# Decode block with adaptive norm: the last weights cut into five transfers, and the first norm worked in columns

## The chip, the cores and the metric

The kernel runs on one core of one Trainium2 chip. The metric is the device time of one execution in microseconds (us): 699.27 us before the change, the median of three runs (698.72 to 700.05). All data is float32. The four compute engines are called PE (TensorE, matrix products), DVE (VectorE), ACT (ScalarE) and POOL (GpSimd); SP (SyncE) issues the transfers.

## The reference

One decode step (one new token) for a batch of two: attention over a cache of 4096 positions with 32 heads of width 128, then a two-layer network with the Mish activation. Each half stands behind a layer norm whose shift, scale and output gate come from a condition `c`.

```python
mod = (_silu(c) @ w_mod).reshape(c.shape[0], 6, 1, -1)
sa, ca, ga, sb, cb, gb = (mod[:, i] for i in range(6))
h = _layernorm(x) * (1 + ca) + sa
x = x + ga * _A_ref(h, k_cache, v_cache, wq, wo)   # softmax(q k / sqrt(128)) v, then wo
h = _layernorm(x) * (1 + cb) + sb
x = x + gb * _B_ref(h, w1, b1, w2)                 # mish(h w1 + b1) w2
```

The caches are 2 x 32 x 4096 x 128 numbers each, 268 of the 297 MB that the kernel reads. `w_mod` is 512 x 3072, `wq` 512 x 4096, `wo` 4096 x 512, `w1` 512 x 1376 and `w2` 1376 x 512.

## The kernel before

**Transfers.** All large loads are issued by SP into three rooms of 64 KB per partition (tag `room0` to `room2`), which take turns. The first is `first` (L83): the modulation's weights for five of the six vectors and the bias `b1`. Then come `wq` (L86), the keys of head 0 (L87), 31 transfers for the heads (L89 to L95; most hold the keys of one head and the values of an earlier one), `wo` (L97), the values of heads 29 and 30 in the room named `two` (L102), then `last` (L107: the values of head 31 in two parts, the rest of `wo`, and `w1` in two halves), and at the end `tail` (L123). `tail` holds the weights of the output gate's modulation `gb` and those of the second layer, `w2`, in 11 chunks of 128 rows; it comes in four transfers, in the order of `src["w2"]`: the gate's modulation with chunks 0 to 4, chunks 5 to 7, chunks 8 and 9, and chunk 10 (`_lay_out`, L635 to L639). A room is loaded again as soon as its last reader is through: `used` (L152) issues the next entry of `plan` when what it holds has been read. The room of `tail` is that of `two`, so its issue waits for the value product of head 30 (`values(H - 2)`, L486). A small transfer `cx` (L73) brings condition and input as 16 rows of 128 numbers on ACT's queue, beside `first`.

**Start.** Two products with an identity (L264, L267) turn `cx` into columns (feature on the partition, `cps`) and into rows at a spacing of 32 partitions (`xq`). The condition goes through silu into `ct` (L269 to L273). The first norm works on rows, with its mean and variance summed over partitions by two products with `mean_w` (`centred`, `rstd`, L204 to L229). `modulation` (L236) multiplies `ct` with the weights in `first`: three vectors (L284), then two (L291). Scale and shift are applied on rows (L286, L287), and `columns` turns the result into `ht` (L288). The queries follow when `wq` is there (L308).

**Heads.** For each head DVE multiplies keys by the query (L336) and sums (L340), PE and ACT do the softmax over partitions, and PE multiplies the weights with the values (L382) in the accumulators `ov`.

**End.** After the last head's values, `wo` is applied (L491), the second norm and the first layer run (L502 to L546), and the hidden layer collects in `fps` (L559). Then PE's order is: the gate's modulation (L568), four products that keep PE busy and whose result nobody reads (`idle(4)`, L569), and 44 products of the second layer in the order of the chunks (L585). DVE and ACT make the activation `actt` from `fps` meanwhile (L572 to L580), multiply the result `yps` by the gate (L593) and add the residual (L594), and SP stores it.

```python
    x2_rows = keep("x2", x2ps)
    gps = modulation("5", 0, 1, w_t["mod5"])
    idle(4)
```

Of the kernel before, what the change touches and what calls it, by code (L numbers as in the profile page):

```python
# [8 lines left out]
F32 = mybir.dt.float32  # L9
BF16 = mybir.dt.bfloat16  # L10
# [4 lines left out]
P = 128  # L15
B = 2
# [14 lines left out]
WO_FIRST = H - 2  # L31

# [12 lines left out]
def kernel(ctx: ExitStack, tc: tile.TileContext, src: dict, out: bass.AP):  # L45
# [26 lines left out]
    cx = const.tile([16, P], F32, name="cx")  # L72
    nc.scalar.dma_start(out=cx, in_=src["cx"])  # L73

# [10 lines left out]
    b1_early = first[:, G * 5 * D :]  # L85
# [66 lines left out]
    def used(*items):  # L152
# [37 lines left out]
    busy = const.tile([P, 512], BF16, name="busy")  # L190
    for t in (ct, ht, h2t, x2t, *(t for pair in e_t for t in pair), busy):
        nc.gpsimd.memset(t, 0.0)
# [11 lines left out]
    def centred(s):  # L204
        rs = const.tile([P, 8], F32, name="rs")
        xc = const.tile([P, P], F32, name="xc")
        sq = const.tile([P, P], F32, name="sq")
        nc.vector.tensor_reduce(out=rs[:, 0:1], in_=s, axis=AX.X, op=ALU.add)
        mps = small_ps("mean_a")
        nc.tensor.matmul(mps[:, 0:1], lhsT=mean_w, rhs=rs[:, 0:1], start=True, stop=True)  # L210
        nc.vector.tensor_scalar(out=xc, in0=s, scalar1=mps[:, 0:1], scalar2=None, op0=ALU.subtract)
        nc.vector.scalar_tensor_tensor(
            sq, xc, 1.0, xc, op0=ALU.mult, op1=ALU.mult, accum_out=rs[:, 1:2]
        )
        vps = small_ps("var_a")
        nc.tensor.matmul(vps[:, 0:1], lhsT=mean_w, rhs=rs[:, 1:2], start=True, stop=True)
        return xc, vps[:, 0:1], rs

    def rstd(var, rs):
        nc.scalar.activation(rs[:, 2:3], var, AF.Ln, bias=eps_t[:, 0:1])  # L220
        nc.vector.tensor_scalar(out=rs[:, 4:5], in0=var, scalar1=EPS, scalar2=None, op0=ALU.add)
        nc.scalar.activation(rs[:, 3:4], rs[:, 2:3], AF.Exp, scale=-0.5)
        nc.vector.scalar_tensor_tensor(
            rs[:, 5:6], rs[:, 3:4], rs[:, 4:5], rs[:, 3:4], op0=ALU.mult, op1=ALU.mult
        )
        nc.vector.tensor_scalar(
            out=rs[:, 5:6], in0=rs[:, 5:6], scalar1=-0.5, scalar2=1.5, op0=ALU.mult, op1=ALU.add
        )
        return rs[:, 3:4], rs[:, 5:6]  # L229
# [28 lines left out]
    def idle(n):  # L258
        for _ in range(n):
            nc.tensor.matmul(ov[1], lhsT=busy[:, 0:P], rhs=busy, start=True, stop=True)  # L260


    cps = small_ps("cps")[:, : 2 * G * B]
    nc.tensor.matmul(cps, lhsT=cx, rhs=ident[0:16, 0 : 2 * G * B], start=True, stop=True)  # L264
    cps, xtps = (cps[:, G * B * i : G * B * (i + 1)].rearrange("p (g b) -> p g b", b=B) for i in range(2))
    xps0 = small_ps("xps0")[:, :P]
    nc.tensor.matmul(xps0, lhsT=place.rearrange("p g r -> p (g r)"), rhs=cx, start=True, stop=True)  # L267
    sg = const.tile([P, G, B], F32, name="sg")
    nc.scalar.activation(sg, cps, AF.Exp, scale=-1.0)  # L269
    nc.vector.tensor_scalar(out=sg, in0=sg, scalar1=1.0, scalar2=None, op0=ALU.add)  # L270
    nc.vector.reciprocal(sg, sg)
    nc.vector.tensor_tensor(out=ct[:, :, 0:B], in0=cps, in1=sg, op=ALU.mult)
    nc.vector.tensor_copy(two(ct)[:, :, B - 1], ct[:, :, B - 1])  # L273
    xt = small("xt")
    nc.vector.tensor_copy(xt, xtps)
    xq = const.tile([P, P], F32, name="xq")
    nc.vector.tensor_copy(xq, xps0)

    xn = const.tile([P, P], F32, name="xn")
    xc, var, rs = centred(xq)  # L280
    y0, y1 = rstd(var, rs)
    nc.vector.tensor_scalar(out=xn, in0=xc, scalar1=y0, scalar2=y1, op0=ALU.mult, op1=ALU.mult)

    ps = modulation("0", 0, 3, w_t["mod"])  # L284
    hq = const.tile([P, P], F32, name="hq")
    nc.vector.scalar_tensor_tensor(hq, ps[:, 1, :], 1.0, xn, op0=ALU.add, op1=ALU.mult)  # L286
    nc.vector.tensor_tensor(out=hq, in0=ps[:, 0, :], in1=hq, op=ALU.add)  # L287
    hps = columns(hq, "hps")  # L288
    nc.vector.tensor_copy(ht[:, :, 0:B], hps)
    ga = keep(2, ps[:, 2, :])  # L290
    ps = modulation("3", 3, 2, w_t["mod"])  # L291
    sb, cb = keep(3, ps[:, 0, :]), keep(4, ps[:, 1, :])
    gat, cbt, scale_t = small("gat"), small("cbt"), small("scale_t")
# [174 lines left out]
    def whole(t, name):  # L468
        ps = small_ps(name)[:, : G * B]
        nc.tensor.matmul(ps, lhsT=ones, rhs=t, start=True, stop=True)  # L470
        s = const.tile([P, B], F32, name=name)
        nc.vector.tensor_reduce(
            out=s, in_=over_g(ps.rearrange("p (g b) -> p g b", b=B)), axis=AX.X, op=ALU.add
        )
        return s

# [12 lines left out]
    for i in range(2):  # L489
# [11 lines left out]
    u, x2, xm, sq2 = small("u"), two(x2t), small("xm"), small("sq2")  # L501
    nc.vector.tensor_tensor(out=u, in0=xps, in1=scale_t, op=ALU.mult)  # L502
    nc.vector.tensor_tensor(out=h2t[:, :, 0:B], in0=u, in1=offset, op=ALU.add)
    nc.vector.tensor_tensor(out=xm, in0=xps, in1=gat, op=ALU.mult)
    nc.vector.tensor_tensor(out=x2, in0=xm, in1=xt, op=ALU.add)
    x_sum = whole(x2, "x_sum")
    nc.vector.scalar_tensor_tensor(
        xm, each_g(x_sum), -1.0 / D, x2, op0=ALU.mult, op1=ALU.add
    )
    nc.vector.tensor_tensor(out=sq2, in0=xm, in1=xm, op=ALU.mult)  # L510
# [16 lines left out]
    v_sum = whole(sq2, "v_sum")  # L527
    for k in range(1, G):
        first_layer(k)
    st = const.tile([P, 6, B], F32, name="st")  # L530
    nc.scalar.activation(st[:, 0], v_sum, AF.Ln, bias=eps_t[:, 0:1], scale=1.0 / D)
    nc.scalar.activation(st[:, 1], st[:, 0], AF.Exp, scale=-0.5)
    nc.vector.tensor_scalar(
        out=st[:, 2], in0=v_sum, scalar1=-0.5 / D, scalar2=-0.5 * EPS, op0=ALU.mult, op1=ALU.add
    )
    nc.vector.scalar_tensor_tensor(st[:, 3], x_sum, 1.0 / D, near, op0=ALU.mult, op1=ALU.subtract)
    coef = small("coef")
# [123 lines left out]
```

## Time and profile before

| | before |
|---|---|
| median of three runs | 699.27 us (698.72 to 700.05) |
| the profiled execution, its own time | 698.93 us |
| its span, first to last instruction | 697.2 us |
| read from memory | 297.23 MB, 426 GB/s over the span |
| DVE busy | 587.6 us (84%) |
| PE busy | 292.9 us (42%) |
| ACT, POOL busy | 39.5 us (6%), 4.7 us (1%) |

The span is the time between the first and the last instruction of the profiled execution. The run's own time has 1.7 us more, which lie around the span. A busy share is a mean over the whole span; where the end of the kernel is set by one chain of work, the chain and the stretch around it say more than the share. Bytes in transit are shown as the mean busy share of the core's 16 DMA engines.

### The profile page before, as it was taken

What the parts mean: (1) busy time and instruction counts of PE and PEld (TensorE: products, weight loads), DVE (VectorE), ACT (ScalarE), POOL (GpSimd) and SP (SyncE); (2) the same over time, 40 slices, a digit from 0 to 9 for tenths busy, and PEclk for the clock granted to TensorE, in tenths of its full rate; (3) what the DMA queues carried; (4) which work ended last, traced back from release to release, by engine and by line L of the source; (5) the groups of instructions that cost most, each with busy time, mean ns of one, the idle gap of its engine ahead of it and who ended that gap; (6) DMA issues with size and microseconds to landing.
All of it is one profiled execution on the core that took longest, in us unless ns stands there. A gap on an engine that the chain in (4) does not pass through costs nothing.

```text
span 697.2 us, 4054 instructions
## 1 busy us (share of the span) xinstructions
PE 292.9 (42%) x1679; PEld 100.6 (14%) x1680; DVE 587.6 (84%) x240; ACT 39.5 (6%) x187; POOL 4.7 (1%) x22
## 2 busy tenths in 40 slices
PE   2360435432350435443504453444322453443886
PEld 1110101110110101111101111111100111110244
DVE  3039999999899999999999999999999899999102
ACT  1000000000000000000000000000000000000000
POOL 2000000000000000000000000000000000000000
PEclk9775565666655666566655558665765566556879
DMA  9999999999999999999999999999999999999996
GB/s 407 406 448 425 432 456 429 422 429 440 445 429 425 426 440 440 432 430 416 446 440 430 432 432 437 432 429 440 429 433 432 426 440 432 433 432 413 434 418 252
DMA packets 6686, 297.49 MB, mean 427 GB/s; under 512 B 756, under 2 KB 780, under 8 KB 1292
## 3 DMA queue, kind: packets, MB, share of 16 engines
q1 hardware_dynamic: 6636, 297.23, 98.8%
q8 instruction: 13, 0.21, 0.1%
q14 instruction: 5, 0.04, 0.0%
q10 hardware_dynamic: 32, 0.01, 0.0%
HBM read 297.23 MB, written 0.00 MB: 426 GB/s over the span
## 4 chain that ended last, share of the span: by engine, by line
DMA 49%; DVE 45%; PE 5%; issue 0%; ACT 0%; SPq 0%; DVEq 0%
DMA kv<-in_pair 40%; DVE kv L336 22%; DVE s L340 21%; DMA two<-in_single 4%; PE ov L382 2%; DMA tail<-in_w 2%; DMA first<-in_mod 2%; PE modps L241 1%; DVE n L358 1%; DVE n L357 1%; PE yps L585 0%; PE otp L398 0%; PE att L422 0%; PE last_ps L463 0%; DVE m L350 0%
## 5 line engine op out<-in xcount | busy, mean ns | idle before, releaser
L336 DVE TENSOR_TENSOR kv<-kv,qb 128x8192 f32<-128x8192 f32 x32 | 277.9, 8684 | 44.2 <-DMA kv<-in_pair 22.5
L340 DVE TENSOR_REDUCE s<-kv 128x64 f32<-128x8192 f32 x32 | 277.4, 8667 | 0.0
L382 PE MATMUL ov<-kv,e 128*32 128x512 f32 x928 | 168.6, 893 | 5.2 <-ACT e L366 5.2
L362 PE MATMUL mb<-n,ones 2*128 2x2 f32 x64 | 17.7, 344 | 221.4 <-DVE n L358 221.4
L321 PE MATMUL qb<-q_sb,row_of 32*128 32x512 f32 x32 | 28.4, 1035 | 65.4 <-DVE kv L336 65.4
L382 PEld LDWEIGHTS ov<-kv,e 128*32 128x32 f32 x928 | 36.9, 156 | 118.7 <-issue 109.6
L362 PEld LDWEIGHTS mb<-n,ones 2*128 2x128 f32 x64 | 15.8, 303 | 230.3 <-issue 155.5
L352 PE MATMUL mt<-ident,m 128*2 128x128 f32 x64 | 13.7, 300 | 75.8 <-DVE m L350 75.8
L363 ACT COPY m<-mb 128x2 f32<-128x2 f32 x32 | 5.1, 160 | 532.2 <-PE mb L362 423.7
L366 ACT ACTIVATE e<-s,m 128x32 f32<-128x32 f32 x64 | 20.0, 314 | 1.2
L321 PEld LDWEIGHTS qb<-q_sb,row_of 32*128 32x128 f32 x32 | 8.8, 302 | 73.7 <-DVE kv L336 67.8
L352 PEld LDWEIGHTS mt<-ident,m 128*2 128x2 f32 x64 | 3.1, 82 | 97.4 <-DVE m L350 76.7
L410 DVE RECIPROCAL total<-l 128x8 f32<-128x8 f32 (+1 forms) x9 | 1.7, 184 | 14.7 <-PE l L408 14.7
L308 PE MATMUL qps<-wq,ht 128*32 128x512 f32 x64 | 9.5, 761 | 10.5 <-DMA wq<-in_wq 10.5
L366 ACT ACTIVATION_READ_ACCUMULATOR e<-s,m 128x1 f32 x64 | 11.9, 186 | 0.0
L398 PE MATMUL otp<-pick,o 128*128 128x8 f32 (+1 forms) x72 | 9.5, 258 | 3.9 <-ACT o L394 3.9
L382 PE MATMUL ov<-two,e 128*32 128x512 f32 x64 | 9.7, 763 | 0.3 <-DMA two<-in_single 0.3
L422 PE MATMUL att<-wo,ot 128*2 128x512 f32 x60 | 9.6, 742 | 0.4 <-DVE ot L401 0.3
L398 PEld LDWEIGHTS otp<-pick,o 128*128 128x128 f32 x72 | 8.7, 191 | 5.5 <-ACT o L394 5.5
L401 DVE TENSOR_TENSOR ot_last<-otp,total 128x4 f32<-128x4 f32 x1 | 0.2, 163 | 11.0 <-PE otp L398 11.0
L357 DVE TENSOR_REDUCE n<-mt 2x1 f32<-2x128 f32 x32 | 8.7, 272 | 0.5 <-PE mt L352 0.5
L394 ACT COPY o<-ov 128x512 f32<-128x512 f32 x9 | 5.3, 586 | 61.4 <-PE ov L382 61.4
(140 smaller groups left out, 107.2 us busy)
## 6 DMA issues: line engine op xcount, KB each, us to landing
kv<-in_single SPq DMA_DIRECT2D x3, 4096.0 KB, 31.1
two<-in_single SPq DMA_DIRECT2D x2, 4096.0 KB, 34.3
wo<-in_wo SPq DMA_DIRECT2D x1, 7680.0 KB, 39.1
first<-in_mod SPq DMA_DIRECT2D x1, 5132.0 KB, 15.1
last<-in_single SPq DMA_DIRECT2D x1, 3072.0 KB, 27.6
last<-in_w SPq DMA_DIRECT2D x2, 1376.0 KB, 34.7
tail<-in_w SPq DMA_DIRECT2D x1, 2304.0 KB, 16.2
last<-in_single SPq DMA_DIRECT2D x1, 1024.0 KB
```

Of the source, the lines that this page charges most:

```text
L241: nc.tensor.matmul(ps[R * g : R * (g + 1)], lhsT=ct[:, k, :], rhs=t[:, k, :].rearrange("p (m n) -> p m n", m=n)[:, :, P * g : P * (g + 1)] ...
L308: nc.tensor.matmul(ps[R * g : R * (g + 1)], lhsT=ht[:, k, :], rhs=w_t["wq"][:, k, 512 * c : 512 * (c + 1)], start=(k == 0), stop=(k == G - 1),
L321: nc.tensor.matmul(qb[:, b], lhsT=row_of[R * g : R * (g + 1), b], rhs=q_sb[R * g : R * (g + 1), half], start=True, stop=True,)
L336: nc.vector.tensor_tensor(out=k_t[h], in0=k_t[h], in1=qv, op=ALU.mult)
L340: nc.vector.tensor_reduce(out=s_t[h].rearrange("p b j -> p (b j)"), in_=k_t[h].rearrange("p b j d -> p (b j) d"), axis=AX.X, op=ALU.add,)
L352: nc.tensor.matmul(mps[h], lhsT=m_t[h][:, 0:2], rhs=ident, start=True, stop=True)
L357: nc.vector.tensor_reduce(out=n[:, 0:1], in_=mps[h], axis=AX.X, op=ALU.max, negate=True)
L362: nc.tensor.matmul(bps[:, 0:2], lhsT=ones[0:B, :], rhs=n[:, 1:3], start=True, stop=True)
L366: nc.scalar.activation(e_t[h % 4][b][:, :, lo : lo + 4], s_t[h][:, b].rearrange("p (c m) -> p c m", m=4), AF.Exp, bias=m[:, 2 + b : 3 + b] ...
L382: nc.tensor.matmul(ov[i % 2][R * g : R * (g + 1), :], lhsT=e_t[h % 4][b][:, c, :], rhs=v_t[h][:, b, 4 * c : 4 * c + 4, :].rearrange("p m d ...
L398: nc.tensor.matmul(tps[:, :n], lhsT=o[:, m, :], rhs=pick[:, m, at : at + n], start=(m == 0), stop=(m == 3))
L422: nc.tensor.matmul(att[R * g : R * g + B, :], lhsT=ot[:, B * h : B * (h + 1)], rhs=w_t["wo"][:, h, :], start=(h < G), stop=(h >= H - 2 - G),)
```

## The change

Three things are changed. (1) Condition and input are laid out as 16 columns of `first`; `cx`, its two products and the row tiles go, and POOL copies those columns and `b1` out of the room into `early`. The first norm is done on columns with the helpers that the second norm now shares, and both modulations run before it. (2) `tail` comes in five transfers instead of four: the gate's modulation alone, chunks 0 to 5, chunks 6 to 8, chunk 9 and chunk 10. Chunk 9 is stored in memory as 8 blocks of 17 rows, of which 16 are read, so that its slowest dimension is 8. (3) The four products of `idle(4)` go.

```diff
-    cx = const.tile([16, P], F32, name="cx")
-    nc.scalar.dma_start(out=cx, in_=src["cx"])
...
-    b1_early = first[:, G * 5 * D :]
+    early_in = first[:, G * 5 * D :]
...
         for part in src["w2"]:
+            if len(part.shape) == 3:
+                nc.sync.dma_start(out=t[:, lo : lo + D], in_=part)
+                lo += D
+                continue
             load(t, lo, part)
...
+    def centred(x, x_sum, name):
+        xm, sq = small(f"xm_{name}"), small(f"sq_{name}")
+        nc.vector.scalar_tensor_tensor(xm, each_g(x_sum), -1.0 / D, x, op0=ALU.mult, op1=ALU.add)
+        nc.vector.tensor_tensor(out=sq, in0=xm, in1=xm, op=ALU.mult)
+        return xm, sq
...
+    early = const.tile([P, (NJ + 2) * G * B], F32, name="early")
+    nc.gpsimd.tensor_copy(early, early_in)
+    c_in, xt = (early[:, G * B * i : G * B * (i + 1)].rearrange("p (g b) -> p g b", b=B) for i in range(2))
+    b1 = early[:, 2 * G * B :]
+    sg = small("sg")
+    nc.scalar.activation(sg, c_in, AF.Exp, scale=-1.0)
...
     ps = modulation("0", 0, 3, w_t["mod"])
+    mod = [keep("012", ps)]
     ps = modulation("3", 3, 2, w_t["mod"])
+    mod.append(keep("34", ps))
+
+    h, sq = centred(xt, whole(xt, "x_sum_a"), "a")
+    times_root(root(whole(sq, "v_sum_a"), "a"), h)
+    nc.vector.scalar_tensor_tensor(h, columns(mod[0][:, 1], "caps"), 1.0, h, op0=ALU.add, op1=ALU.mult)
+    nc.vector.tensor_tensor(out=ht[:, :, 0:B], in0=columns(mod[0][:, 0], "saps"), in1=h, op=ALU.add)
...
     gps = modulation("5", 0, 1, w_t["mod5"])
-    idle(4)
...
+    def on_low_engines(w):
+        t = np.zeros((LOW, P // LOW + 1, w.shape[-1]), w.dtype)
+        t[:, : P // LOW] = w.reshape(LOW, P // LOW, -1)
+        return t
...
-        "cx": np.ascontiguousarray(np.concatenate([eight(a["c"]), eight(a["A_x"])])),
-        "mod01234": join(wm[:, :, : 5 * D], b1c),
+        "mod01234": join(wm[:, :, : 5 * D], eight(a["c"]), eight(a["A_x"]), b1c),
...
-        "w2_0": join(wm[:, :, 5 * D :], w2[:, :5]),
-        "w2_1": join(w2[:, 5:8]),
-        "w2_2": join(w2[:, 8:10]),
-        "w2_3": join(w2[:, 10:]),
+        "w2_0": join(wm[:, :, 5 * D :]),
+        "w2_1": join(w2[:, :6]),
+        "w2_2": join(w2[:, 6:9]),
+        "w2_3": on_low_engines(w2[:, 9]),
+        "w2_4": join(w2[:, 10:]),
...
+    src["w2"][3] = src["w2"][3][:, : P // LOW]
```

At the start, PE before the change stands as follows, from the first product to the last one ahead of the queries (`modps` are the two modulations, `hps` the normed input as columns, `gaps`, `cbps`, `sbps` three modulation vectors as columns).

```order
L264 MATMUL cps<-ident,cx 128x16
L267 MATMUL xps_129<-cx,place 128x128
L210 MATMUL mean_a<-rs,mean_w 128x1
L216 MATMUL var_a<-rs,mean_w 128x1
L241 MATMUL modps_158<-first,ct 32x384 x16
L233 MATMUL hps<-ident,hq 128x8
L241 MATMUL modps_183<-first,ct 32x256 x16
L233 MATMUL gaps<-ident,mod_181 128x8
L233 MATMUL cbps<-ident,mod_202 128x8
L233 MATMUL sbps<-ident,mod_200 128x8
```

After the change the same place has nine groups.

```order
L235 MATMUL modps_126<-first,ct 32x384 x16
L235 MATMUL modps_145<-first,ct 32x256 x16
L197 MATMUL x_sum_a<-early,ones 128x8
L197 MATMUL v_sum_a<-sq_a,ones 128x8
L227 MATMUL caps<-ident,mod_143 128x8
L227 MATMUL saps<-ident,mod_143 128x8
L227 MATMUL gaps<-ident,mod_143 128x8
L227 MATMUL cbps<-ident,mod_162 128x8
L227 MATMUL sbps<-ident,mod_162 128x8
```

The four products ahead of the modulation are gone, and the two sums of the first norm and its two vectors as columns (`caps`, `saps`) now follow both modulations.

At the end, PE before the change stands as follows from the last product of the first layer (`busy` stands four times in a row, and three are left out).

```order
L517 MATMUL w1ps<-last,h2t 32x256
L550 MATMUL x2ps<-ident,x2t 32x128 x4
L559 MATMUL last_ps<-coef,last 128x8 x3
L241 MATMUL modps_1575<-tail,ct 32x128 x16
L260 LDWEIGHTS busy
L260 MATMUL ov_126<-busy 128x512
...
L585 MATMUL yps<-tail,last 32x128 x44
```

After the change:

```order
L485 MATMUL w1ps<-last,h2t 32x352
L485 MATMUL w1ps<-last,h2t 32x256
L508 MATMUL x2ps<-ident,x2t 32x128 x4
L517 MATMUL last_ps<-coef,last 128x8 x3
L235 MATMUL modps_1561<-tail,ct 32x128 x16
L542 MATMUL yps<-tail,last 32x128 x44
```

The gate's modulation (`modps`) stays behind the hidden layer's products (`last_ps`), and the second layer (`yps`) follows it at once.

On SP, the last loads stood so before; a name in brackets that begins with DMAHW is one of eight completion semaphores that the loads use in turn, so a wait on it is a wait for the load eight places earlier (and, on `tail_0`, for the room).

```order
L69 DMA last<-in_w 128x2752 x2
L69 DMA tail<-in_w_0 128x4608 [waits DMAHW4_49,DMAHW5_49,DMAHW3_49,PE_49]
L69 DMA tail<-in_w_1 128x1536
L69 DMA tail<-in_w_2 128x1024
L69 DMA tail<-in_w_3 128x512 [waits DMAHW6_49]
L595 DMA out<-y 4x2x128 [waits DMAHW7_49,DVE_49]
```

After the change:

```order
L69 DMA last<-in_w 128x2752 x2
L69 DMA tail<-in_w_0 128x2048 [waits DMAHW3_49,DMAHW4_49,DMAHW2_49,PE_49]
L69 DMA tail<-in_w_1 128x3072
L69 DMA tail<-in_w_2 128x1536
L127 DMA tail<-in_w_3 128x1x512 [waits DMAHW5_49]
L69 DMA tail<-in_w_4 128x512 [waits DMAHW6_49]
L552 DMA out<-y 4x2x128 [waits DMAHW7_49,DVE_49]
```

There is one issue more. The fourth load of `tail` (chunk 9) waits for the first part of `last`, as the fourth did before; the fifth waits for the second part of `last`, which the store `out` waited for before.

## Rows read from the trace of the kernel before

**Rows 1.** Page, slices of the span and the chain that ended last

```profile
DMA  9999999999999999999999999999999999999996
...
DMA 49%; DVE 45%; PE 5%; issue 0%; ACT 0%; SPq 0%; DVEq 0%
```

**Rows 2.** Page, costliest groups: line, busy and mean, idle before and releaser

```profile
L336 DVE TENSOR_TENSOR kv<-kv,qb 128x8192 f32<-128x8192 f32 x32 | 277.9, 8684 | 44.2 <-DMA kv<-in_pair 22.5
```

**Rows 3.** Timeline, start: start us, us, instruction, [idle before <-releaser]

```profile
7.49 0.18 ACT L269 ACTIVATE sg<-cps 128x8 f32<-128x8 f32 x1 [5.04 <-PE cps L264]
...
8.44 0.17 DVE L273 COPY ct<-ct 128x4 f32<-128x4 f32 x1
...
15.85 0.20 POOL L300 COPY b<-first 128x24 f32<-128x24 f32 x1 [11.46 <-DMA first<-in_mod]
...
15.93 4.68 PE L241 MATMUL modps<-first,ct 128*32 128x384 f32 x32 [4.72 <-DMA first<-in_mod]
```

**Rows 4.** Timeline, SP's first issue for a pair, and the query product

```profile
23.72 0.33 SPq L69 DMA_DIRECT2D kv<-in_pair  x1
...
35.30 9.53 PE L308 MATMUL qps<-wq,ht 128*32 128x512 f32 x64 [10.53 <-DMA wq<-in_wq]
```

**Rows 5.** Timeline, second norm: a sum over partitions and its reduction

```profile
683.37 0.60 PE L470 MATMUL v_sum<-sq,ones 128*128 128x8 f32 x2
...
684.00 0.17 DVE L472 TENSOR_REDUCE v_sum<-v_sum 128x2 f32<-128x8 f32 x1 [1.37 <-PE v_sum L470]
```

**Rows 6.** Chain of waits from 660 us on: start us, us, what

```profile
672.92 16.16 DMA tail<-in_w
...
689.22 1.08 PE modps L241 x32
...
690.46 0.81 PE ov L260 x3
691.27 2.58 PE yps L585 x88
...
693.95 0.30 DVE y L593
```

**Rows 7.** Tile tail, its four issues: ns min/median/max, first and last start

```profile
L69 SPq DMA_DIRECT2D tail<-in_w x4: 327/422/430, 672.9 to 674.2; - x4
```

**Rows 8.** DMA issues of the tail: KB each, us from issue to landing

```profile
tail<-in_w SPq DMA_DIRECT2D x1, 2304.0 KB, 16.2
...
tail<-in_w SPq DMA_DIRECT2D x1, 768.0 KB, 17.6
...
tail<-in_w SPq DMA_DIRECT2D x1, 512.0 KB, 18.4
...
tail<-in_w SPq DMA_DIRECT2D x1, 256.0 KB, 18.6
```

**Rows 9.** Waits of SP's queue from 660 us on: us in total, times, longest

```profile
SPq L595 <- DMA last<-in_single: 1.0, 1, 1.0
```

**Rows 10.** Timeline, hidden layer: last product and last activation step

```profile
687.32 0.83 PE L559 MATMUL last_ps<-coef,last 128*128 128x8 f32 x6 [0.34 <-ACT last L556]
...
689.58 0.20 DVE L580 TENSOR_TENSOR last<-f 128x22 f32<-128x22 f32 x1
```

**Rows 11.** Windows: PE, PEld, DVE, ACT, POOL busy (x), PEclk, DMA share, GB/s

```profile
690.60:691.00 0.40, 0.40 (x3) 0.10 (x1) 0.00 (x0) 0.03 (x1) 0.00 (x0) 1.00 0.25 102
...
692.20:692.60 0.40, 0.40 (x24) 0.40 (x20) 0.00 (x0) 0.00 (x0) 0.00 (x0) 1.00 0.03 10
```

**Rows 12.** Page, instruction queue: packets, MB, share of 16 engines

```profile
q8 instruction: 13, 0.21, 0.1%
```

**Rows 13.** DMA queues from 681 to 683.5 us, the same columns

```profile
q8 instruction: 1, 0.02, 2.7%
```

**Rows 14.** Windows as in rows 11, two stretches by granted clock

```profile
681.99:685.40 3.41, 3.41 (x24) 1.71 (x27) 1.74 (x12) 0.50 (x2) 0.00 (x0) 0.50 1.00 424
685.40:697.20 11.80, 6.84 (x153) 5.15 (x145) 1.88 (x9) 1.24 (x6) 0.00 (x0) 1.00 0.41 165
```

More of the change, by code (lines that the diff above doesn't have):

```diff
@@ L189 @@
     ot_last = const.tile([P, 2 * B], F32, name="ot_last")
-    busy = const.tile([P, 512], BF16, name="busy")
-    for t in (ct, ht, h2t, x2t, *(t for pair in e_t for t in pair), busy):
+    for t in (ct, ht, h2t, x2t, *(t for pair in e_t for t in pair)):
         nc.gpsimd.memset(t, 0.0)
@@ L219, in rstd, with whole @@
[L219 to L224, printed above, removed]
-        )
[L226 to L229, printed above, removed]
+    def whole(t, name):
+        ps = small_ps(name)[:, : G * B]
+        nc.tensor.matmul(ps, lhsT=ones, rhs=t, start=True, stop=True)
+        s = const.tile([P, B], F32, name=name)
+        nc.vector.tensor_reduce(
+            out=s, in_=over_g(ps.rearrange("p (g b) -> p g b", b=B)), axis=AX.X, op=ALU.add
+        )
+        return s
@@ L231, in columns, with times_root @@
+    def times_root(st, t):
+        for _ in range(2):
+            nc.vector.tensor_tensor(out=st[:, 2], in0=st[:, 2], in1=st[:, 1], op=ALU.mult)
+        nc.vector.tensor_tensor(out=t, in0=t, in1=each_g(st[:, 1]), op=ALU.mult)
+        nc.vector.scalar_tensor_tensor(t, each_g(st[:, 2]), 1.5, t, op0=ALU.add, op1=ALU.mult)
     def columns(s, name):
@@ L256, in small @@
         return const.tile([P, G, B], F32, name=name)
[L258 to L267, printed above, removed]
@@ L271 @@
     nc.vector.reciprocal(sg, sg)
-    nc.vector.tensor_tensor(out=ct[:, :, 0:B], in0=cps, in1=sg, op=ALU.mult)
+    nc.vector.tensor_tensor(out=ct[:, :, 0:B], in0=c_in, in1=sg, op=ALU.mult)
     nc.vector.tensor_copy(two(ct)[:, :, B - 1], ct[:, :, B - 1])
[L274 to L281, printed above, removed]
@@ new lines @@
+    h, sq = centred(xt, whole(xt, "x_sum_a"), "a")
+    times_root(root(whole(sq, "v_sum_a"), "a"), h)
+    nc.vector.scalar_tensor_tensor(h, columns(mod[0][:, 1], "caps"), 1.0, h, op0=ALU.add, op1=ALU.mult)
+    nc.vector.tensor_tensor(out=ht[:, :, 0:B], in0=columns(mod[0][:, 0], "saps"), in1=h, op=ALU.add)
+    gat, cbt, scale_t = small("gat"), small("cbt"), small("scale_t")
+    nc.vector.tensor_copy(gat, columns(mod[0][:, 2], "gaps"))
+    nc.vector.tensor_scalar(
+        out=cbt, in0=columns(mod[1][:, 1], "cbps"), scalar1=1.0, scalar2=None, op0=ALU.add
+    )
@@ L466 @@
         )
[L468 to L475, printed above, removed]
     xa, offset = small("xa"), small("offset")
@@ L498 @@
             )
-    u, x2, xm, sq2 = small("u"), two(x2t), small("xm"), small("sq2")
+    u, x2, xg = small("u"), two(x2t), small("xg")
     nc.vector.tensor_tensor(out=u, in0=xps, in1=scale_t, op=ALU.mult)
     nc.vector.tensor_tensor(out=h2t[:, :, 0:B], in0=u, in1=offset, op=ALU.add)
[L504 to L510, printed above, removed]
+    nc.vector.tensor_tensor(out=xg, in0=xps, in1=gat, op=ALU.mult)
+    nc.vector.tensor_tensor(out=x2, in0=xg, in1=xt, op=ALU.add)
+    x_sum = whole(x2, "x_sum_b")
+    _, sq = centred(x2, x_sum, "b")
     w1ps = wide_ps("w1ps")
@@ L526 @@
     first_layer(0)
-    v_sum = whole(sq2, "v_sum")
+    v_sum = whole(sq, "v_sum_b")
     for k in range(1, G):
         first_layer(k)
[L530 to L535, printed above, removed]
+    st = root(v_sum, "b")
     nc.vector.scalar_tensor_tensor(st[:, 3], x_sum, 1.0 / D, near, op0=ALU.mult, op1=ALU.subtract)
@@ L654 @@
         ).ap()
-    src["w2"] = [src.pop(f"w2_{i}") for i in range(4)]
+    src["w2"] = [src.pop(f"w2_{i}") for i in range(5)]
+    src["w2"][3] = src["w2"][3][:, : P // LOW]
     out = nc.dram_tensor("out", inputs["A_x"].shape, F32, kind="ExternalOutput").ap()
```

57 lines of the change are left out of this document (12 added, 45 removed).

## The prediction

> **What bounds the kernel now.** I read the page first: the DMA engines are busy in every slice of the span but the last, and the chain that ended last alternates between transfers (49%) and DVE (45%) [rows 1]. Of the two the transfers set the pace: DVE's product over the keys stood idle 44.2 us in all, most of it until a pair had landed [rows 2]. So what leaves the number of bytes alone can only gain or lose at the two ends: before the queue is full, and after it begins to run dry. The next view is the timeline of the start. The modulation begins at 15.93, as soon as `first` has landed, and the queries only at 35.30, when `wq` has landed; PE is idle for 10.53 us before that [rows 3, 4]. The start therefore has room. The last view is the chain at the end: `tail` is issued at 672.92, its first transfer lands 16.16 us later at 689.08, the gate's modulation starts at 689.22 (0.14 us from landing to product), the four unread products hold PE until 691.27, the second layer takes 2.58 us and the multiplication by the gate starts at 693.95, 0.10 us behind the last product [rows 6]. Everything after that is the same in both kernels.
>
> **The start, part by part.** Removed are `cx`, its two products and the row tiles, all before `first` lands: nothing. The condition now arrives with `first`. POOL copies it at 15.85 in 0.20 us (40 columns for 24, taken at the same price). From the start of the exponential to the end of the copy into `ct` it took 7.49 to 8.61, 1.12 us [rows 3]. So the modulation starts at about 17.3 in place of 15.93, 1.4 us late. Both modulations and the release of the room took from 15.93 to 23.72 [rows 3, 4]; the next pair is thus issued at 25.1 instead of 23.72. The queue then still holds the rest of `wq`, which lands only at about 35.2, and the keys of head 0 behind it, so DMA does not notice. The norm on columns follows: two sums over partitions at 0.80 us each (683.37 to 684.17 [rows 5]), and some 12 small steps of DVE and ACT, 0.3 us each with their gaps at the most, 3.6 us. `ht` is ready near 25.1 + 1.6 + 3.6 = 30.3, 5 us ahead of `wq`. Were PE at half its clock all the way, 3 to 4 us more would still fit. I cost the start at 0.0; its cover is the wait for `wq`, and behind that DVE's waits for pairs [rows 2]. The bytes of `cx` move into `first` and are 8 KB either way: 0.0.
>
> **The end, part by part.** First the price of bytes there. The four issues stand 0.43 us apart (672.9 to 674.2 [rows 7]). With the times to landing [rows 8] the four land at 689.1, 673.35 + 17.6 = 690.95, 673.8 + 18.4 = 692.2 and 674.2 + 18.6 = 692.8. 768 KB thus take 1.85 us, or **0.62 us for 256 KB** on 16 engines.
>
> - The gate's weights alone are 1280 KB less than the first transfer before: they land at 689.1 - 5 x 0.62 = 686.0. The hidden layer's products end at 688.15 (687.32 + 0.83 [rows 10]), so the gate's modulation no longer waits and runs from 688.2 to 689.3, in the shade of the activation on DVE, which ends at 689.78 [rows 10].
> - `idle(4)` goes: with its gap before it 0.97 us of PE's time ahead of the second layer (690.30 to 691.27 [rows 6]).
> - Chunks 0 to 5 end 256 KB later than the first transfer did: 689.1 + 0.62 = 689.7. The second layer starts at about 689.85, both operands being there within 0.1 us of one another. A chunk takes 2.58 / 11 = 0.235 us.
> - Chunks 6 to 8 end 768 KB further: 691.6. PE is through with chunk 5 at 691.26, so here is the **new wait**: chunk 6 starts at 691.6 + 0.14 = 691.74, and everything behind it moves with it.
> - Chunk 9, on eight engines, costs these 16 rows in place of 8, 1.24 us, and the other eight nothing. Chunk 10 costs all 0.62 us.
>
> What chunk 9 does depends on which engines are last. Their ends are apart: from 690.6 to 691.0 the mean share is 0.25, work for four of 16, and from 692.2 on it is 0.03 [rows 11]. So a few engines end up to 1.5 us after the rest. One reason shows: 13 blocks of instructions of 16 KB each came through the same engines [rows 12], and one of them held its engine for 2.7% of 16 x 2.5 us, 1.08 us [rows 13]; 13 delays can't be even on 16 engines. No row names the engines. If the late ones are among the eight without chunk 9, chunk 10 lands there at 691.6 + 0.62 = 692.2, and chunk 9 on the others at 691.6 - 1.4 + 1.24 = 691.4; neither is waited for (they are due at 692.45 and 692.68). If the late ones have chunk 9, it lands at 692.8 and chunk 10 at 693.5. These are the two ends of the cost: no wait, or 0.9 us. The rows say this much: on one engine 13 blocks would make 14 us, so they rotate; in a rotation over all 16 none would get more than one, and a lag of 1.5 us is more than one block of 1.08 us. So the rotation seems to pass over fewer engines, perhaps one half of them, some of which got two blocks and the other half none. Which half that is, no row says. I take the one without chunk 9; that is a choice, and its odds are set below.
>
> - Sum: 691.74 + 5 x 0.235 = 692.92, + 0.10 = 693.02 for the gate's product, against 693.95: **0.93 us less**.
>
> The profiled execution (698.93 us) would so take 698.0. The median of the runs shown, 699.27, lies 0.34 us above it; I set the forecast against the median: 698.3.
>
> Two waits are added on SP. The fourth issue waits for the first part of `last`, as before. The fifth waits for its second part, which ended the 1.0 us wait of `out` behind the fourth issue before [rows 9], at about 675.7. Only `out` is queued behind it, and the queue has work until 691: 0.0; it would cost only if that part landed after 691.
>
> [...] No row before shows a transfer on fewer than 16.
>
> **Rivals.**
>
> 1. *The doubled engines are the late ones.* Chunk 10 lands at 693.5, starts at 693.6, and the gate's product at 693.6 + 0.235 + 0.10 = 693.95: nothing gained, **699.3**. For it: every one of the late engines must lie in the half without chunk 9, or its lag counts, and four drawn at random would seldom do so. Against it: a lag of more than one block speaks for a rotation over a part of the engines [rows 11, 13]. [...] Chance 0.28.
> 2. *Slower: the clock falls without the four products.* They were wide and stood right ahead of the second layer. [...] If it falls again before 689.85, the second layer takes 2 x 2.58 = 5.16 us, ends at 695.0, and the gate's product is at 695.1: 1.2 us more, **700.4**. It decides if the clock is 0.5 for over half of the second layer; from 691.74 on it would cost 1.2 us for five chunks and eat up the gain. Against it: PE had nothing to do from 688.15 to 689.22 before, and the clock held; that gap is now filled, and the new ones are 0.5 us. Chance 0.08.
> 3. *Chunk 9 is spread over all 16 after all.* All lands at 692.8 as before, chunk 10 starts at 692.94, the product is at 693.27: 0.68 us less, **698.6**. Chance 0.08.
>
> **How the numbers follow.** A measurement of this kernel can tell about 0.2%, 1.4 us, from no change. The forecast, 698.3, has 0.49; its own range is 697.8 to 698.8, from chunks 6 to 8 landing 0.4 us earlier or later and the scatter of the medians. Another 0.07 is for what I don't see. The second layer can't start before the activation at 689.78, so the most to be had is 693.95 - (689.85 + 2.58 + 0.10) = 1.4 us; that is why faster by over 0.2% has only 0.13. Slower by over 0.2% needs rival 2 with an unlucky scatter: 0.07. The rest, 0.80, is within 0.2%. For 8 in 10 the range takes in rivals 1 and 3 with their scatter and leaves out rival 2: 697.6 to 699.9.
>
> **What would show it.** In the changed kernel's profile: the modulation near 17.3, `ht` before 31, the query product still at 35.3; the gate's modulation at 688.2 without a wait for DMA; the second layer from 689.85 with a wait for `tail` in its middle and none at its end; the gate's product near 693.0, with the clock at 1.0 in the 3 us before it; fewer engines idle before 691. A wait at the second layer's end is rival 1, a layer of 5 us rival 2. The forecast is wrong if the transfers themselves end at another time, if the queries move, or if the second layer starts after 690.5.

## The result, and the profile after

The change makes the kernel slower by an amount that only many runs can tell: 700.47 us (699.49 to 702.14, 20 runs) against 698.87 us for the kernel before on the same chip (698.61 to 700.50, 20 runs), a ratio of 1.0019 with an interval of 1.0012 to 1.0026. The forecast was 698.3 with a range up to 699.9. The profiled execution took 700.56 us and its span 698.8 us; before it was 698.93 and 697.2, so the profile carries the same 1.6 us as the medians. The times of both kernels fall into two groups, before at 698.4 to 699.3 us (93 of 126 executions in all) and 700.0 to 700.6, after at 699.5 to 699.7 (6 of 20) and 700.2 to 702.1, and the two profiles are of unlike groups: between like ones the loss is 0.4 to 0.7 us, and the rest is that more executions fall into the upper group.

The page's lines on engines, instruction queue, bytes and the chain that ended last:

```profile
PE 290.4 (42%) x1674; PEld 100.1 (14%) x1674; DVE 585.3 (84%) x235; ACT 39.7 (6%) x186; POOL 4.3 (1%) x21
...
q8 instruction: 13, 0.21, 0.1%
...
HBM read 297.23 MB, written 0.00 MB: 425 GB/s over the span
...
DMA 55%; DVE 42%; PE 2%; issue 0%; ACT 0%; SPq 0%; POOL 0%; DVEq 0%
```

The bytes and the 13 blocks of instructions are the same as before [rows 12]. The chain is now 55% transfers, where it was 49% [rows 1]: it ends in a transfer, where the old one ended in PE's work. The timeline, first at the start, then from the issue of `tail` on (start us, us, instruction, idle before and its releaser):

```profile
16.11 0.22 POOL L254 COPY early<-first 128x40 f32<-128x40 f32 x1 [12.21 <-DMA first<-in_mod]
...
17.60 6.37 PE L235 MATMUL modps<-first,ct 128*32 128x384 f32 x64 [17.60 <-DVE ct L262]
...
24.07 20.32 SPq L69 DMA_DIRECT2D kv<-in_pair  x2
...
27.14 0.17 DVE L272 TENSOR_TENSOR ht<-saps,xm_a 128x8 f32<-128x8 f32 x1
...
35.46 8.53 PE L288 MATMUL qps<-wq,ht 128*32 128x512 f32 x64 [7.34 <-DMA wq<-in_wq]
...
672.03 1.28 SPq L69 DMA_DIRECT2D tail<-in_w  x3
673.44 0.79 SPq L127 DMA_DIRECT2D tail<-in_w  x1
...
675.95 0.33 SPq L69 DMA_DIRECT2D tail<-in_w  x1
...
688.69 0.83 PE L517 MATMUL last_ps<-coef,last 128*128 128x8 f32 x6 [0.35 <-ACT last L514]
...
689.46 1.08 PE L235 MATMUL modps<-tail,ct 128*32 128x128 f32 x32
...
690.96 0.20 DVE L537 TENSOR_TENSOR last<-f 128x22 f32<-128x22 f32 x1
...
691.26 1.52 PE L542 MATMUL yps<-tail,last 128*32 128x128 f32 x48 [0.72 <-DVE last L537]
...
693.22 0.86 PE L542 MATMUL yps<-tail,last 128*32 128x128 f32 x24 [0.44 <-DMA tail<-in_w]
...
694.39 0.43 PE L542 MATMUL yps<-tail,last 128*32 128x128 f32 x8 [0.31 <-DMA tail<-in_w]
...
695.04 0.43 PE L542 MATMUL yps<-tail,last 128*32 128x128 f32 x8 [0.23 <-DMA tail<-in_w]
...
695.61 0.29 DVE L550 TENSOR_TENSOR y<-yps,mod 128x128 f32<-128x128 f32 x1 [4.45 <-PE yps L542]
```

At the start the modulation begins 1.7 us later than before [rows 3], `ht` is ready at 27.3, and the queries still wait for `wq` until 35.46 [rows 4]. At the end the second layer stops three times for `tail`: ahead of chunk 6 (693.22), of chunk 9 (694.39) and of chunk 10 (695.04). Before it ran in one piece of 2.58 us [rows 6]. The gate's product comes at 695.61, 1.66 us later, which is the whole difference between the two profiled executions.

The DMA issues of `tail` (KB each, us from issue to landing):

```profile
tail<-in_w SPq DMA_DIRECT2D x1, 1536.0 KB, 18.4
...
tail<-in_w SPq DMA_DIRECT2D x1, 1024.0 KB, 14.3
tail<-in_w SPq DMA_DIRECT2D x1, 768.0 KB, 20.3
...
tail<-in_w SPq DMA_DIRECT2D x2, 256.0 KB, 19.0
```

With the first three issues at 672.03, about 672.46 and about 672.9, the gate lands at 686.3, chunks 0 to 5 at 690.9 and chunks 6 to 8 at 693.2. Chunk 10 lands at 675.95 + 19.05 = 695.00 by the chain of waits. Before, the last of the same bytes were there at 692.8 [rows 7, 8]. The windows (columns as in rows 11; the view gives some shares a little over 1) show where the 2.2 us went:

```profile
688.00:688.80 0.80, 0.45 (x9) 0.19 (x4) 0.00 (x0) 0.53 (x4) 0.00 (x0) 1.00 1.09 361
688.80:689.60 0.80, 0.80 (x12) 0.78 (x16) 0.04 (x1) 0.21 (x2) 0.00 (x0) 1.00 0.94 241
689.60:690.40 0.80, 0.80 (x32) 0.67 (x26) 0.47 (x3) 0.22 (x1) 0.00 (x0) 1.00 0.93 241
690.40:691.20 0.80, 0.14 (x8) 0.00 (x0) 0.62 (x4) 0.27 (x1) 0.00 (x0) 1.00 0.69 192
```

Read the last two columns together. From 688.8 to 690.4 the engines are busy for 0.94 of the time, yet they move 241 GB/s: 241 / 0.94 = 256 GB/s for a full share. Before it was 102 / 0.25 = 408 [rows 11]; in the same window of the kernel before it was 343 / 0.85 = 404:

```profile
688.80:689.60 0.80, 0.38 (x16) 0.41 (x20) 0.63 (x5) 0.00 (x0) 0.00 (x0) 1.00 0.85 343
```

At 0.94 the engines are not idle; each packet takes longer. The trace also keeps the length of every packet: from 688.8 to 689.6 the median of those of 2 KB (chunks 9 and 10) is 136 ns, that of those of 6 KB (chunks 6 to 8) 367 ns; in the same 0.8 us of e1, the first run below, it is 84 and 238 ns. And it keeps each step in which the completion of a load counts up, 16 for a plain load. The 16 steps of chunks 0 to 5 come between 686.3 and 690.9. Read as one step for each of the 16 engines, which no row names, they say that the engines don't move together: the first of them are at chunk 9 while the last still carry chunks 0 to 5. That is the theory to test: **chunk 9, in its blocks, slows itself and the other transfers in flight.** The rivals were the doubled engines alone, the padding of the blocks in memory, the start, and the four products taken away.

### The profile page after: what moved, and what is told of

It is laid out like the page before. It is cut to its first block, busy times and chain, and to the rows that moved or that the text cites. A ratio compares the mean times of both kernels' runs of the same rounds, so it can differ in the third digit from the quotient of the medians.

```text
span 698.8 us, 4029 instructions
## 1 busy us (share of the span) xinstructions
PE 290.4 (42%) x1674; PEld 100.1 (14%) x1674; DVE 585.3 (84%) x235; ACT 39.7 (6%) x186; POOL 4.3 (1%) x21
## 4 chain that ended last, share of the span: by engine, by line
DMA 55%; DVE 42%; PE 2%; issue 0%; ACT 0%; SPq 0%; POOL 0%; DVEq 0%
DMA kv<-in_pair 45%; DVE kv L316 21%; DVE s L320 20%; DMA last<-in_single 4%; DMA tail<-in_w 3%; DMA first<-in_mod 2%; PE ov L362 1%; PE modps L235 1%; DVE n L338 1%; DVE n L337 0%; DVE m L330 0%; PE otp L378 0%; ACT o L374 0%; PE mb L342 0%; SPq L69 0%
## 5 line engine op out<-in xcount | busy, mean ns | idle before, releaser
L235 PE MATMUL modps<-first,ct 128*32 128x384 f32 (+1 forms) x64 | 6.4, 564 | 17.6 <-DVE ct L262 17.6
```

Of the source, the lines that this page charges most:

```text
L235: nc.tensor.matmul(ps[R * g : R * (g + 1)], lhsT=ct[:, k, :], rhs=t[:, k, :].rearrange("p (m n) -> p m n", m=n)[:, :, P * g : P * (g + 1)] ...
```

## The experiments

A plain transfer here is one of 128 rows, one for each partition. Rates "for a full share" are the GB/s of a window divided by its DMA share. Each ratio is against the kernel before, timed beside it.

### The blocks undone, and three other ways of writing them

**e1_plain**: the changed kernel with chunk 9 as a plain transfer.

```diff
-        "w2_3": on_low_engines(w2[:, 9]),
+        "w2_3": join(w2[:, 9]),
...
-    src["w2"][3] = src["w2"][3][:, : P // LOW]
```

> The changed kernel with chunk 9 as an ordinary transfer of 128 rows on all 16 engines; all else as changed. Three theories of the loss. Block theory: chunk 9, cut into 8 blocks, makes its engines write where other engines write at the same time, and everything in flight slows down. Doubling theory: the only cost is twice the rows on engines of which one is late. Memory theory: the padded blocks are slow to read. All three expect the loss to go here: rate over share stays near 400 GB/s in the tail (in the changed kernel it falls to about 250 from 688.5 to 690.6), the last transfer lands near 693.1, the gate's product starts near 693.5 in place of 695.6, and the time is 0.3 to 0.8 us below the kernel before (ratio about 0.999). If it stays at 1.002, the cut is not the cause.

Measured: 698.88 us, ratio 0.9997 (0.9988 to 1.0006). The loss is gone (10 of the 11 executions took 698.7 to 699.5 us), but the 0.3 to 0.8 us of gain that was expected does not show. Its timeline at the end:

```profile
688.25 1.08 PE L235 MATMUL modps<-tail,ct 128*32 128x128 f32 x32
...
690.10 1.52 PE L542 MATMUL yps<-tail,last 128*32 128x128 f32 x48 [0.77 <-DMA tail<-in_w]
...
691.89 1.09 PE L542 MATMUL yps<-tail,last 128*32 128x128 f32 x32 [0.28 <-DMA tail<-in_w]
...
693.20 0.43 PE L542 MATMUL yps<-tail,last 128*32 128x128 f32 x8 [0.23 <-DMA tail<-in_w]
...
693.77 0.29 DVE L550 TENSOR_TENSOR y<-yps,mod 128x128 f32<-128x128 f32 x1 [3.82 <-PE yps L542]
```

Two of its windows, as in rows 11:

```profile
688.80:689.60 0.80, 0.53 (x20) 0.26 (x12) 0.70 (x4) 0.20 (x1) 0.00 (x0) 1.00 0.89 353
689.60:690.40 0.80, 0.30 (x12) 0.33 (x16) 0.25 (x2) 0.06 (x1) 0.00 (x0) 1.00 0.71 277
```

A full share moves 353 / 0.89 = 397 GB/s and 277 / 0.71 = 390 GB/s. Against the change's profile, chunk 6 starts 1.33 us earlier and the last chunk 1.84 us. The form of this one transfer is the whole loss. The 1.84 us have two parts. The transfers up to chunk 8 land 1.3 us later in the change. And behind them chunk 9 takes 1.17 us there (its products start at 694.39) and 0.66 us in e1, by the steps of their completion; that is the other 0.5 us.

**e2_blocks16** takes 16 blocks of 9 rows (8 read), for 16 engines in place of eight (no row names an engine; but the completion of chunk 9 counts up in 9 steps in the change and in e3, one of them at its issue, and in 16 in e1 and e2, which fits); **e3_pitch24** keeps 8 blocks but moves them 24 rows apart in memory instead of 17; **e4_halves** has no padding at all and loads chunk 9 in two transfers of 64 partitions.

```diff
-LOW = 8
+LOW = 16
```

> Chunk 9 in 16 blocks of 8 rows (stored in blocks of 9), so that all 16 engines take 8 rows each, and none is doubled. Block theory: rows still go to partitions in runs that are not those of an ordinary transfer, so packets of all transfers beside it still slow down, by less or for a shorter time; the gate's product starts 0.3 to 1.2 us later than with the plain transfer, rate over share dips below 330 GB/s. Doubling theory: the same as the plain transfer within 0.2 us. Memory theory: the dip is there too, as the blocks are padded.

```diff
-        t = np.zeros((LOW, P // LOW + 1, w.shape[-1]), w.dtype)
+        t = np.zeros((LOW, P // LOW + 8, w.shape[-1]), w.dtype)
```

> The changed kernel with the 8 blocks of chunk 9 stored 24 rows apart in place of 17; same engines, same partitions. Block and doubling theory: no difference from the changed kernel, ratio 1.002 against the kernel before, the dip to about 250 GB/s per full share stays, the gate's product starts near 695.6. Memory theory: the dip changes by over a quarter, in depth or length.

```diff
+            if part is src["w2"][3]:
+                for p in (0, P // 2):
+                    nc.sync.dma_start(out=t[p : p + P // 2, lo : lo + D], in_=part[p : p + P // 2])
+                lo += D
+                continue
...
-        "w2_3": on_low_engines(w2[:, 9]),
+        "w2_3": join(w2[:, 9]),
...
```

> Chunk 9 as two ordinary transfers of 64 partitions each, from an unpadded source; every engine still takes 8 rows in all. [...] Doubling and memory theory: the same as the plain transfer within 0.2 us (one more issue is hidden).

Measured: 700.42 (1.0015, 1.0005 to 1.0024), 700.59 (1.0013, 1.0004 to 1.0022) and 700.26 us (1.0012, 1.0003 to 1.0021). All three keep the loss that e1, timed beside them, has not. The window from 688.8 to 689.6 gives 282 GB/s for a full share in e2, 240 in e3 and 275 in e4. These are the windows, in this order:

```profile
688.80:689.60 0.80, 0.74 (x6) 0.74 (x6) 0.00 (x0) 0.39 (x4) 0.00 (x0) 1.00 0.96 271
...
688.80:689.60 0.80, 0.80 (x14) 0.78 (x18) 0.10 (x1) 0.15 (x1) 0.00 (x0) 1.00 0.95 228
...
688.80:689.60 0.80, 0.59 (x7) 0.56 (x6) 0.00 (x0) 0.56 (x4) 0.00 (x0) 1.00 1.09 300
```

In e3's profiled execution, of 699.62 us, the gate's product came at 694.69 and not near 695.6 as expected. The end of its chain of waits (start us, us, what):

```profile
693.26 1.34 PE yps L542 x40
...
694.69 0.30 DVE y L550
```

Chunk 6 starts as late as in the change, but chunks 9 and 10 are not waited for. e3 deals its rows as the change does, so this dealing costs 0.92 us against e1 in one execution and 1.84 us in another. So the loss is not that only eight engines carry the chunk, not the distance of the blocks in memory, and not the padding.

### The other two parts of the change, each alone

**f1_start** has the new start with the four old transfers and the four products; **f2_noidle** is the kernel before without those products.

```diff
...
+    for _ in range(4):
+        nc.tensor.matmul(ov[1], lhsT=busy[:, 0:P], rhs=busy, start=True, stop=True)
...
+        "w2_0": join(wm[:, :, 5 * D :], w2[:, :5]),
+        "w2_1": join(w2[:, 5:8]),
+        "w2_2": join(w2[:, 8:10]),
+        "w2_3": join(w2[:, 10:]),
...
```

> The start of the changed kernel alone: condition and input in the first transfer, first norm on columns; the four transfers of tail and the four unread products as before. By every theory the start is hidden behind the transfer of wq: query product at 35.2 to 35.6, same time as before, ratio within 0.0010 of 1. A ratio of 1.001 or more would put a part of the loss at the start.

```diff
-    idle(4)
```

> The kernel before without its four unread products; nothing else changed. If the products only cost PE time, the second layer starts at 690.4 and then waits for chunks 8 to 10, so the gate's product starts near 693.3 in place of 693.95 and the time is 0.3 to 0.7 us less (ratio 0.999 to 0.9995). If they keep the clock up, the granted clock is 0.5 in the second layer and the time is 1 us more or above (ratio 1.0015).

Measured: f1 699.38 us, 1.0005 (0.9996 to 1.0014); f2 698.73 us, 0.9999 (0.9990 to 1.0008). In f1 the queries start at 35.48; in four kernels with the old start it was 35.30 to 35.76. The start is hidden behind `wq`. f1's median is 0.5 us above the kernel before, and its interval reaches 1.0 us: so much can't be told from nothing. In f2 the granted clock is 1.00 throughout the second layer, as its window shows (columns as in rows 11):

```profile
691.40:694.00 2.60, 2.55 (x88) 2.37 (x88) 0.00 (x0) 0.00 (x0) 0.00 (x0) 1.00 0.10 35
```

The four products did not hold the clock up, and taking them away gained nothing that can be measured. The gate's product was expected near 693.3 and came at 694.18: the second layer waited for the activation until 691.45, as the last product of the hidden layer started at 688.83 and not at 687.32 [rows 10].

### Which partitions are written

If the cost lies in where the engines write, half of chunk 9 can tell: partitions 32 to 95 alone (**m1_middle**), 0 to 63 alone (**m2_lower**), both unpadded transfers of 64 rows, with the rest set to zero by POOL. **d1_own** loads 0 to 63 again, but in padded blocks of four rows, eight blocks to a transfer, two transfers of 32 partitions.

```diff
+                for p, z in ((0, 32), (96, 128)):
+                    nc.gpsimd.memset(t[p:z, lo : lo + D], 0.0)
+                nc.sync.dma_start(out=t[32:96, lo : lo + D], in_=part[32:96])
...
-        "w2_3": on_low_engines(w2[:, 9]),
+        "w2_3": join(w2[:, 9]),
...
```

> As the kernel with chunk 9 plain, but of chunk 9 only the rows of partitions 32 to 95 are loaded; the other half of that chunk is set to zero and left out. 64 rows go to 16 engines, four each. [...] If any transfer of fewer than 128 partitions is slow, the dip is there as with the two halves.

m2 has 0 to 64 in the place of 32 to 96.

> The same with the rows of partitions 0 to 63 instead: the same bytes, the same 16 engines, four rows each. [...] If the count of partitions or of rows is what matters, both runs are alike within 0.2 us.

```diff
+                for i in range(2):
+                    nc.sync.dma_start(out=t[P // 4 * i : P // 4 * (i + 1), lo : lo + D], in_=part[i])
...
-        t = np.zeros((LOW, P // LOW + 1, w.shape[-1]), w.dtype)
-        t[:, : P // LOW] = w.reshape(LOW, P // LOW, -1)
+        t = np.zeros((2, LOW, 5, w.shape[-1]), w.dtype)
+        t[:, :, :4] = w[: P // 2].reshape(2, LOW, 4, -1)
```

> [...] Theory that a cut into blocks or a transfer on eight engines is slow by itself: the dip is there as in the changed kernel, for about half its length.

Measured: 699.00 (0.9999, 0.9988 to 1.0010), 698.99 (1.0000, 0.9991 to 1.0008) and 699.16 us (0.9999, 0.9989 to 1.0008). With 128 KB less to load, the medians don't separate them. The last transfer landed 0.5 us later in m2 (693.4 against 692.9). But in m1's profile the hidden layer was late and the second layer waited for the activation until 691.22, so the gate's product came at 693.96 there and at 693.98 in m2, alike by chance. The windows (columns as in rows 11) do separate them. In m1:

```profile
688.80:689.60 0.80, 0.80 (x14) 0.78 (x18) 0.08 (x1) 0.17 (x2) 0.00 (x0) 1.00 0.76 302
```

In m2:

```profile
688.00:688.80 0.80, 0.80 (x14) 0.78 (x17) 0.12 (x1) 0.13 (x1) 0.00 (x0) 1.00 1.07 361
688.80:689.60 0.80, 0.80 (x32) 0.58 (x24) 0.44 (x4) 0.22 (x1) 0.00 (x0) 1.00 0.84 287
```

In d1:

```profile
688.80:689.60 0.80, 0.80 (x10) 0.78 (x13) 0.00 (x0) 0.32 (x3) 0.00 (x0) 1.00 0.83 328
```

That is 397 GB/s for a full share in m1, 337 and 342 in m2, 395 in d1; in the window from 688.8 to 689.6 the five kernels that write only 128 partitions at a time (before, e1, f1, f2, g2) have 393 to 404. The packets of 2 KB say the same: their median there is 84 ns in m1 and d1, 108 ns in m2. m1 and m2 move as many bytes to as many partitions and differ only in which (and so in which rows of memory they read; d1 reads the rows of m2 without a dip). m2 and d1 write the same partitions and differ in how the rows are dealt out: d1 has padding, blocks and eight engines at a time (its two loads complete in 9 steps each), as the change has, and no dip. So what counts is which partitions a transfer writes and how it deals its rows out. That both come down to which partitions are written at the same time is the simplest reading; no row shows it directly. Nor does a run show why 32 to 95 keep the rate (397) and 0 to 63 don't (337 and 342).

### The same cost elsewhere, and the best of both

**g1_halves_all** loads all five parts of `tail` in halves of 64 partitions; **g3_blocks_alone** is the kernel before with only chunk 10 in the change's blocks; **g2_cut_noidle** has the old start, the five transfers all plain, and no idle products.

```diff
-            load(t, lo, part)
+            for p in (0, P // 2):
+                nc.sync.dma_start(out=t[p : p + P // 2, lo : lo + part.shape[1]], in_=part[p : p + P // 2])
...
-        "w2_3": on_low_engines(w2[:, 9]),
+        "w2_3": join(w2[:, 9]),
...
```

> The suspected cost taken five times: start and cut of the changed kernel, but every one of the five transfers of tail goes in two halves, partitions 0 to 63 and then 64 to 127 (3.9 MB in place of the 0.26 MB of chunk 9). [...] If what costs is only the change from one dealing of rows to the other, or a single odd transfer, the loss stays near the 1.4 us of the run with chunk 9 in halves.

```diff
...
-        "w2_3": join(w2[:, 10:]),
+        "w2_3": on_low_engines(w2[:, 10]),
...
```

> The kernel before with one thing changed: its last transfer, chunk 10, is stored and loaded in 8 blocks of 16 rows. [...] Doubling alone, with packets at 84 ns: the last landing at 693.5 at most, which the second layer hides to within 0.3 us: ratio below 1.0006.

```diff
-    idle(4)
...
+        "w2_0": join(wm[:, :, 5 * D :]),
...
+        "w2_1": join(w2[:, :6]),
+        "w2_2": join(w2[:, 6:9]),
+        "w2_3": join(w2[:, 9]),
+        "w2_4": join(w2[:, 10:]),
...
```

> The part of the change that the runs speak for: start as before, the five transfers all as ordinary ones of 128 rows, no unread products. If the loss is all in the dealing of chunk 9 and the start costs 0.2 us, this is the fastest version: last landing 692.8 to 693.0, the gate's product at 693.4 to 693.8, ratio 0.9985 to 0.9998. If the hidden layer is late (two clock stretches at 0.5), up to 694.2 and a ratio of 1.

Measured: g1 708.47 us, 1.0127 (1.0113 to 1.0142); g3 699.62 us, 1.0004 (0.9995 to 1.0012); g2 699.81 us, 1.0010 (1.0001 to 1.0019). Three windows of g1, as in rows 11:

```profile
688.00:688.80 0.80, 0.80 (x9) 0.50 (x6) 0.00 (x0) 0.00 (x0) 0.00 (x0) 0.50 0.98 220
...
691.40:694.00 2.60, 2.60 (x34) 2.47 (x38) 0.94 (x5) 0.28 (x2) 0.00 (x0) 0.50 0.96 213
...
700.00:702.00 2.00, 2.00 (x45) 2.00 (x41) 0.00 (x0) 0.00 (x0) 0.00 (x0) 0.50 0.16 51
```

The end of its chain of waits (start us, us, what):

```profile
674.43 24.23 DMA tail<-in_w
...
698.80 4.28 PE yps L543 x88
...
703.17 0.30 DVE y L551
```

With half of the partitions at a time a full share moves 224 and 222 GB/s, little over half of 408. The second half of chunks 0 to 5 lands at 698.66, and only then can the second layer start. It runs in one piece, 4.28 us instead of 2.58, with a granted clock of 0.50 in the windows from 698 to 702, while the rest of `tail` still lands: the last window still shows transfers, and the last step of a completion is at 702.23, 9.1 us later than in e1. The loss of 9.4 us lies nearly all in the transfers; it is far above the 1.4 us near which a single odd transfer, or the change of dealing alone, was expected to leave it. It is the clearest sign: the same bytes, the engines as busy, little over half the rate. In g3 the dip is there with the rest of the change absent (274 GB/s at a share of 0.95 from 688.8 to 689.6, 288 for a full share). Its window and the end of its chain of waits:

```profile
688.80:689.60 0.80, 0.47 (x18) 0.50 (x22) 0.66 (x4) 0.00 (x0) 0.00 (x0) 1.00 0.95 274
```

```profile
673.16 19.91 DMA tail<-in_w
...
693.11 0.91 PE yps L589 x24
...
694.11 0.30 DVE y L597
```

The third transfer lands at 693.07 instead of 692.2, and the gate's product comes only 0.16 us later than before [rows 6]: the old second layer is busy with the earlier chunks until then, so the transfer could be 0.9 us late at a cost of 0.16. So the ratio of 1.0004 stays below the 1.0006 expected of doubling alone, and the dip shows in the window only. g2 was expected to be the best version and is not: no version here is shown to beat the kernel before. It differs from e1 only in its start, and why its median lies 0.9 us above e1's is open. Its profile has no dip (330 GB/s at a share of 0.84), but a hidden layer whose last product starts at 689.03, so the second layer waits for the activation until 691.60 and the gate's product comes at 694.33. That is a little past the upper case of its expectation (694.2).

## Why the prediction was wrong

**The failing step** is "Chunk 9, on eight engines, costs these 16 rows in place of 8, 1.24 us, and the other eight nothing." It priced a transfer by the number of rows that an engine carries, and put what the others in flight lose by it at nothing. No run shows the eight engines as such: what the runs show is that chunk 9's completion counts up in 9 steps, one of them at its issue, where a plain load has 16, and that its products start 1.17 us behind those of chunk 6. The runs show too that its price also depends on which partitions it writes and how its rows are dealt out: 256 GB/s for a full share in place of 408, and for every transfer in flight, not for chunk 9 alone. Chunks 0 to 5, which stand ahead of chunk 9 in the queue, landed at 690.9 instead of the forecast 689.7, and chunks 6 to 8 at 693.2 instead of 691.6. What the sum had for chunk 9 itself was near: 1.17 us for 1.24 us forecast. e1 takes the step out, and the sum before it holds: chunks 0 to 5 are there at about 690.0 (689.7 forecast), chunk 6 starts at 691.89 (691.74 forecast).

Point by point:

- *The start costs 0.0*: right. The modulation came at 17.60 (about 17.3 forecast), `ht` before 31, the queries with `wq`. f1's median is 0.5 us up, which its interval (0.9996 to 1.0014) does not tell from nothing.
- *The gate's modulation no longer waits for its weights*: right. They landed at 686.3 (686.0 forecast). It ran at 689.46 instead of 688.2, because the hidden layer itself was 1.4 us later. Two windows by granted clock show what went with it:

```profile
680.15:686.98 6.83, 6.00 (x36) 3.98 (x39) 2.48 (x17) 0.50 (x2) 0.00 (x0) 0.50 1.00 416
686.98:697.22 10.24, 6.44 (x149) 4.58 (x140) 1.72 (x8) 1.24 (x6) 0.00 (x0) 1.00 0.48 152
```

  The stretch at a granted clock of 0.50 was 6.83 us long instead of 3.41 [rows 14]. In the profiles other than g1's, the last product of the hidden layer starts at 687.1 to 687.8 in the four with the short stretch (before, e1, m2, g3) and at 688.6 to 689.0 in the nine with the long one. With blocks g3 has the short one and the change the long one, without them e1 and f1: this does not go with the blocks. It did not set the end of the change, as chunk 6 came only at 693.2.
- *A new wait ahead of chunk 6, none behind it*: half right. There were three waits, and the last one set the end.
- *The late engines lie in the half without chunk 9*: not so in the change's profile. Of the 16 steps of chunks 6 to 8, twelve are there by 691.6 and the last four at 692.4 to 693.2. If each step is one engine's, chunk 9's last step, at 694.3, can only belong to one of those four engines: 16 packets from 691.6 on, even at 136 ns each, would be through by 693.8. Chunk 10's last step comes 0.65 us behind it. In e3's profile, with the same dealing, neither is waited for. So both ends of that choice occur; it was a toss, and the gate's products of the two profiles lie 0.92 us apart. Without blocks chunk 10 lands at 693.16, not 692.2, so no part of the lag of [rows 11] was won even there.
- *The last chunk in a row, 0.235 us*: mis-sized. A chunk that comes alone takes 0.47 us from its first product's start to its last one's end, in the change and in e1.
- *Rival 1* (the doubled engines are the late ones, 699.3) had the sign of a wait at the second layer's end right, and its doubling is about 0.5 of the 1.84 us between the change and e1. It can't be the cause of the rest: e2 has no doubled engines (its chunk 9 completes in 16 steps), and its median is as high as the change's. *Rival 2* (the clock falls, 700.4) has the number nearest to the 700.47 measured, by luck: it is refuted by f2 and by the 1.00 in the windows above. Its doubling of the layer at a clock of 0.50 was too much besides: in g1's window from 700 to 702, at 0.50, 45 products take 2.00 us, 44 ns each, against 29 ns (2.58 us for 88). *Rival 3* (all 16) is refuted by the 9 steps in which chunk 9 completes; e1 is the kernel that it describes, and took 698.88 for its 698.6.

Even without the blocks the new cut gives little: in e1 the gate's product comes at 693.77 against 693.95, 0.18 us, not the 0.68 us of rival 3. The last landing is 0.36 us later than 692.8 (f1, with the four old transfers, has 693.1 as well), and the last chunk, now alone behind it, takes 0.24 us more. A gain of 0.18 us is less than the timings of this kernel can tell.

Three things stay open: what parts the two groups of times, and why more of the change's fall into the upper one; why the low-clock stretch is long in one execution and short in another; and g2's median. Whether reading the blocks from memory costs anything by itself was not tried apart from d1, which reads padded blocks at the full rate. Each rate of a window is from one profile; from 688.8 to 689.6 the dip is in those of the change, e2, e3, e4, m2, g1 and g3, and in none of the other seven.

## What to carry to other kernels

Beside other transfers the plain form with all 128 partitions was the safe one here: 393 to 404 GB/s for a full share from 688.8 to 689.6. Of the other forms m1 and d1 kept the rate (397 and 395), and the rest had 342 or less. Before a transfer is cut by partitions or dealt to fewer engines, ask which partitions are written at the same time, not only how many rows each engine has. To see such a cost, divide the rate of a short window by its DMA share: here a share near 1 at a lower rate (241 GB/s at 0.94) went with longer packets (136 ns for 2 KB in place of 84), and a falling share whose quotient held (277 GB/s at 0.71) with a queue that ran dry. And take more than one profile of a kernel: two executions with the same dealing, those of the change and e3, differed by 0.92 us at the gate's product. And price a small last piece by its whole path from landing to the end of its own products, not by its share of a long row.

## What the hardware showed that was not expected

One 256 KB transfer, under 0.1% of the bytes, lowered the rate of everything in flight beside it, transfers ahead of it in the queue among them: for a full share 256 and 259 GB/s from 688.8 to 690.4, where e1 had 397 and 390, and 278 from 690.4 to 691.2, where e1 had 351 (207 at a share of 0.59). Halves of 64 partitions ran at 222 to 224 GB/s for a full share when they were 0 to 63 and 64 to 127 in turn (g1). Half a chunk to partitions 32 to 95 ran beside the others at 397, where one to 0 to 63 gave 337 to 342.
